# Linear attention and a GELU layer on one core: batch 3 in quarters, batch 2's x later, and four small reads ahead on ScalarE's DMA queue

## The chip, the core and the metric

The kernel runs on one core of a Trainium2 chip. The core has a matrix engine (TensorE, called PE in the profile, with its weight loads in a row of their own, PEld), VectorE (DVE), ScalarE (ACT), GpSimd (POOL) and SyncE (SP). SP issues nearly all DMA transfers; sixteen DMA engines carry them out. The metric is the device time of one execution in microseconds (us). Before the change the median of three runs is 287.24 us (287.09 to 288.22).

## The reference

The inputs q, k and v are [8 batches, 8 heads, 576 rows, 64], the weights are w_in [512, 2048] and w_out [2048, 512], all float32.

```
q_s = softmax(q) over its last axis
k_s = softmax(k) over the 576 rows
kv  = k_s^T v                      # per batch and head, 64 x 64
x   = (q_s kv), heads side by side # 4608 x 512
out = gelu(x w_in) w_out           # exact gelu, 4608 x 512
```

A softmax of numbers drawn at a tenth of a normal needs no maximum subtracted here: the kernel takes exp and divides by the sum.

## The kernel before

**Tiles.** The first 512 rows of a batch are a chunk; the 64 rows that are left of each of the eight batches make a ninth chunk. So there are nine chunks c = 0 to 8 of 512 rows. For each, `h_phase(c)` computes h = x w_in in sixteen groups t of four 128x512 matmuls (L376), each followed by a gelu on ACT (L381) into g. `y_phase(c)` computes g w_out: four output tiles j, each a sum over sixteen t (L386), copied out of PSUM by DVE (L393) and stored by SP. These matmuls are bf16 and keep PE busy; everything else is placed among them.

**What goes in front of a chunk.** `exp_q` and `exp_k` take exponentials on ACT; `table` loads ACT's function table for exp or gelu. `norm_q` divides q by its sums (DVE sums and reciprocals, POOL and DVE products). `xbar_step` transposes q with a DMA issued by SP, into qT (for batches 0 and 1 PE does it). `cast_v_all` turns v into bf16 on DVE. `kv_step` computes k_s^T v on PE for two head pairs and writes it, divided by the sums, into `kvbd[b]`, 128x128 per head pair with the two heads' blocks on the diagonal. Then x = q_s kv is computed transposed, for four head pairs hp:

- `x_step(b, hp)`: one 128x512 matmul against the 128x128 block (L323) and one evacuation from PSUM into xT, by DVE (L356) or, when told "s", by ACT (L358).
- `x_quad(b)`, for batches from QB on: eight matmuls of 64x64 blocks (L346), which work on quarters of PE's array, then four evacuations. It needs neighbouring head pairs in swapped order, so for those batches the exponentials (`exp_heads`) are four instructions instead of one, each for every fourth head. It uses two accumulators of psum_a and both of psum_y.

With QB = 4, batches 2 and 3 use `x_step`, batches 4 to 7 `x_quad`. The ninth chunk (b = B) mixes the remainders of all batches; its q tile holds two batches in each of four slots, and `exp_main` treats the slots of the batches below QB plainly and the others in four instructions.

**Order.** The order of instructions on each engine is written out by hand: `h_phase` and `y_phase` take a table of small pieces of work to issue after a given t, or after a given (j, t). `h_phase` also takes `groups`: {0: 2} lets the first two groups run side by side, so that each part of xT is read twice before the next is needed. Batch 2's attention is issued within y_phase(1), batch 3's norm, cast and transpose (`front3`) in h_phase(2) after t = 0, its kv_steps after t = 8 and 9 and its x_steps after t = 12 to 15. From batch 4 on the kv_steps stand at t = 1 and 2 and the quad at t = 9 of the phase before.

**Start and end.** SP issues the loads in order: q, k and v of batch 0, w_in in ten transfers, w_out, then batches 1 and 2. Meanwhile 30 matmuls on zeros (`warm`) run on PE. The transfers, of whatever queue, take eight completion semaphores in turn, so each waits until the one eight places ahead has landed. The last output tile (`y_last`) is stored in two column ranges, each half by SP and half by ACT; these two are the only transfers on ACT's queue.

Of the kernel before, what the change touches and what calls it, by code (L numbers as in the profile page):

```python
# [8 lines left out]
FP32 = mybir.dt.float32  # L9
BF16 = mybir.dt.bfloat16  # L10
AF = mybir.ActivationFunctionType
# [5 lines left out]
def kernel(  # L17
# [16 lines left out]
    nc = tc.nc  # L34
# [5 lines left out]
    R = S - M  # L40
    HP = H // 2
    NDM = DM // 128
    NDF = DF // 128
    QB = 4
    PW = 2 * D + 1
    PA = 2 * D + 2
    NS = S // 64
# [2 lines left out]
    singles = ctx.enter_context(tc.tile_pool(name="singles", bufs=1))  # L50
# [50 lines left out]
    def load_main(b, name, t, parts=1):  # L101
        f = f32in.tile([128, 2048 if name == "q" else 2560], FP32, tag=name + "f")
        f = f[:, 0:2048].rearrange("p (h f) -> p h f", h=H)
        st[b][name + "f"] = f
        src = t[b, :, 0:M, :].rearrange("h (p j) d -> p h (j d)", j=J)
        n = H // parts
        for i in range(parts):
            nc.sync.dma_start(out=f[:, i * n:(i + 1) * n, :], in_=src[:, i * n:(i + 1) * n, :])  # L108

    def load_pair(b, name, t, parts):  # L110
        f = f32in.tile([128, 2560], FP32, tag=name + "f")
        f = f[:, 0:HP * NS * D].rearrange("p (x f) -> p x f", x=HP)
        st[b][name + "f"] = f
        src = t[b].rearrange("h (p n) d -> (h p) (n d)", n=NS).rearrange("(x q) f -> q x f", q=128)
        n = HP // parts
        for i in range(parts):
            nc.sync.dma_start(out=f[:, i * n:(i + 1) * n, :], in_=src[:, i * n:(i + 1) * n, :])  # L117
# [9 lines left out]
    def load(b):  # L127
        load_main(b, "q", q)
        load_both(b, "k", k)
        load_both(b, "v", v)  # L130
# [11 lines left out]
    def exp_heads(b, dst, src):  # L142

        if b < QB:
            nc.scalar.activation(out=dst, in_=src, func=AF.Exp)  # L145
            return
        for s, u in ((0, 0), (1, 1), (2, 3), (3, 2)):
            nc.scalar.activation(out=dst[:, s::4], in_=src[:, u::4], func=AF.Exp)  # L148

    def exp_main(b, name, parts=1):  # L150
        if name == "q":
            e = attn_sb.tile([128, J, H, D], BF16, tag="eq")
        else:
            e = ek_main[b % 2]
        st[b]["e" + name] = e
        if b == B:
            f = st[b][name + "f"]
            nc.scalar.activation(out=e[:, 0:QB // 2], in_=f[:, 0:QB // 2], func=AF.Exp)
            for s, u in ((0, 0), (1, 1), (2, 3), (3, 2)):
                nc.scalar.activation(  # L160
                    out=e[:, QB // 2:, s::4], in_=f[:, QB // 2:, u::4], func=AF.Exp
                )
            return
        src = st[b][name + "f"].rearrange("p h (j d) -> p h j d", j=J)
        dst = e.rearrange("p j h d -> p h j d")
        n = H // parts
        for i in range(parts):
            exp_heads(b, dst[:, i * n:(i + 1) * n], src[:, i * n:(i + 1) * n])

    def exp_q(b, parts=1):  # L170
        exp_main(b, "q", parts)

    def exp_k(b, parts=1):
        exp_heads(b, ek_r[b % 2][0:R], st[b]["kr"])
        exp_main(b, "k", parts)
# [84 lines left out]
    def kv_step(b, hps):  # L260
# [7 lines left out]
        for hh in range(2):  # L268
            pr = slice(hh * 64, hh * 64 + 64)
            for i in range(n):  # L270

                c = hh ^ (hps[i] % 2 if b >= QB else 0)
                nc.vector.tensor_scalar_mul(  # L273
# [31 lines left out]
    def xbar_step(b):  # L305
        st[b]["qT"] = attn_sb.tile([128, J, HP, 128], BF16, tag="qT", name="qT")
        nc.sync.dma_start_transpose(
            out=st[b]["qT"].rearrange("p j x m -> p (j x) m"),
            in_=st[b]["eq"].rearrange("p j h d -> p (j h d)"),
        )  # L310
    def x_step(b, hp, eng="v"):
        x_mm(b, hp)
        x_evac(b, hp, eng)

    def x_mm(b, hp):

        pool, tag = (psum_y, "y") if b == 0 else (psum_a, "a")
        if hp == 0:
            st[b]["xT"] = attn_sb.tile([128, HP, M], BF16, tag="xT", name="xT")
        ps = pool.tile([128, M], FP32, tag=tag)  # L320
        st[b][f"x{hp}"] = ps
        if b < B:
            nc.tensor.matmul(ps, kvbd[b][:, hp, :], st[b]["qT"][:, :, hp, :], start=True, stop=True)  # L323
        else:
            for bb in range(B):
                cs = slice(bb * R, (bb + 1) * R)
                s2 = slice(bb % 2 * R, (bb % 2 + 1) * R)
                nc.tensor.matmul(
                    ps[:, cs], kvbd[bb][:, hp, :], st[b]["qT"][:, bb // 2, hp, s2],
                    start=True, stop=True,  # L330
                )

    def x_quad(b, engs="vvvv"):


        st[b]["xT"] = attn_sb.tile([128, HP, M], BF16, tag="xT", name="xT")
        for hp in range(HP):
            pool, tag = (psum_a, "a") if hp < 2 else (psum_y, "y")
            st[b][f"x{hp}"] = pool.tile([128, M], FP32, tag=tag, name="ps")
        for half in range(2):  # L340
            for r in range(2):
                for i in range(2):
                    hp = 2 * half + i
                    pr = slice(r * 64, r * 64 + 64)
                    c = slice((r ^ i) * 64, (r ^ i) * 64 + 64)
                    nc.tensor.matmul(  # L346
                        st[b][f"x{hp}"][c, :], kvbd[b][pr, hp, c], st[b]["qT"][pr, :, hp, :],
                        start=True, stop=True,
                    )
        for hp in range(HP):  # L350
            x_evac(b, hp, engs[hp])

    def x_evac(b, hp, eng="v"):
        ps = st[b][f"x{hp}"]
        if eng == "v":
            nc.vector.tensor_copy(out=st[b]["xT"][:, hp, :], in_=ps)  # L356
        else:
            nc.scalar.copy(out=st[b]["xT"][:, hp, :], in_=ps)  # L358

    def h_phase(c, ins, groups={}, pre={}):  # L360


        g = moe_sb.tile([128, NDF, M], BF16, tag="g", bufs=1)
        st[c]["g"] = g
        xT = st[c]["xT"]
        t1 = 0
        while t1 < NDF:
            t0, t1 = t1, t1 + groups.get(t1, 1)
            ts = range(t0, t1)
            pss = [psum_h.tile([128, M], FP32, tag="h", name="ps") for t in ts]  # L370
            for dm in range(NDM):
                if t0 == 0:
                    for f in pre.get(dm, []):
                        f()
                for ps, t in zip(pss, ts):
                    nc.tensor.matmul(  # L376
                        ps, wi_bf[:, dm, t * 128:(t + 1) * 128], xT[:, dm, :],
                        start=(dm == 0), stop=(dm == NDM - 1),
                    )
            for ps, t in zip(pss, ts):  # L380
                nc.scalar.activation(out=g[:, t, :], in_=ps, func=AF.Gelu)  # L381
                for f in ins.get(t, []):
                    f()
# [92 lines left out]
            nc.tensor.matmul(ps, zeros[:, 0:128], zeros, start=True, stop=True)  # L476


    load_main(0, "q", q, 2)
    load_pair(0, "k", k, 2)  # L480
    load_pair(0, "v", v, 4)
# [74 lines left out]
    def y_end(j):  # L556
# [35 lines left out]
        (1, 12): [lambda: kv_step(2, (0, 1))],  # L592
        (2, 2): [lambda: kv_step(2, (2, 3))],
        (1, 15): [lambda: xbar_step(2)],
        (3, 3): [lambda: x_step(2, 0)],
        (3, 6): [lambda: x_step(2, 1)],
        (3, 9): [lambda: x_step(2, 2)],
        (3, 12): [lambda: x_step(2, 3)],
    })


# [1 line left out]
    def back(b, late=False):  # L603
        s = {}
        if b < B:
            s[8 if late else 1] = [lambda: kv_step(b, (0, 1))]
            s[9 if late else 2] = [lambda: kv_step(b, (2, 3))]
        if QB <= b < B:
            s[9] = [lambda: x_quad(b)]
        else:  # L610
            for hp in range(HP):
                s[(12 if late else 8) + hp] = [lambda hp=hp: x_step(b, hp)]
        return s
# [8 lines left out]
    for c in range(2, B + 1):  # L622
        ins = back(c + 1, c == 2) if c < B else {}
        nb = c + 2
        if c == 2:
            ins[0] = [front3]
        elif nb <= B:
            ins.setdefault(0, []).append(
                (lambda nb=nb: load(nb)) if nb < B else (lambda: load_qrest())
            )  # L630
        h_phase(c, ins)
        yi = {}
        if nb <= B:
            exp_q(nb)
            if nb < B:
                exp_k(nb)
            table(AF.Gelu)
            yi[(1, 0)] = [lambda nb=nb: norm_q(nb)]
            if nb == 4:
                yi[(3, 4)] = [lambda: cast_v_all(4)]  # L640
            elif nb < B:
                yi[(0, 8)] = [lambda nb=nb: cast_v_all(nb)]
            yi[(3, 0)] = [lambda nb=nb: xbar_step(nb)]
        y_phase(c, yi)
# [30 lines left out]
```

The softmax here doesn't subtract the row's maximum and nothing guards it: scores larger than these inputs give would overflow.

## Time and profile before

| What | Value |
|---|---|
| median of three runs | 287.24 us (287.09 to 288.22) |
| the profiled execution's own time | 288.38 us |
| its span (first to last instruction) | 286.5 us |
| PE busy | 278.7 us, 97% |
| granted TensorE clock | 1.00 |
| ACT busy | 157.1 us, 55% |
| DVE busy | 120.2 us, 42% |
| HBM read and written | 36.70 MB, 9.44 MB |

The profile is of one execution. Its span leaves 1.9 us of that execution's time outside. A busy time says how long an engine had at least one instruction in hand; PE's matmuls overlap, so its rate is read from the distance of their starts. Where a line names a releaser ("<-"), that is what ended the idle time before the instruction.

### The profile page before, as it was taken

The page shows a single profiled execution, that of the slowest core. Times are in us where ns is not written, and L with a number is a line of the kernel's source. Part 1 is how long each engine was busy: PE and PEld are TensorE (multiplying, and loading weights), DVE is VectorE, ACT ScalarE, POOL GpSimd, SP SyncE. Part 2 cuts the span into 40 slices and gives each one's busy share as a digit, 9 for nine tenths or more (in the row PEclk, how much of TensorE's full clock was granted, in tenths as well). Part 3 has the DMA queues.
Part 4 walks back from the last instruction along what each step waited for, and adds up shares of the span by engine and source line. Part 5 has one row for each costly group of instructions (what it writes and reads, how often), then busy time and mean ns, then how long its engine had stood idle before and what let it go on. Part 6 is the DMA issues. An engine that isn't in the chain of part 4 may idle for free.

```text
span 286.5 us, 3845 instructions
## 1 busy us (share of the span) xinstructions
PE 278.7 (97%) x1507; PEld 131.3 (46%) x1507; DVE 120.2 (42%) x240; ACT 157.1 (55%) x251; POOL 38.5 (13%) x34
## 2 busy tenths in 40 slices
PE   8989999999899999999999999999999999999994
PEld 3534454445345445444544454445444444444443
DVE  7564387128595555345422632363235112110012
ACT  5777684779355843685268625771665165017400
POOL 5730032002020050005000400041002200000000
PEclk9999999999999999999999999999999999999999
DMA  7999999999809929932995189716701600120033
GB/s 233 375 383 385 373 388 296 293 283 244 161 37 251 297 97 233 258 115 76 214 266 146 73 190 264 172 73 160 136 0 72 147 2 0 73 76 0 0 73 76
DMA packets 58465, 50.05 MB, mean 175 GB/s; under 512 B 26576, under 2 KB 48336, under 8 KB 58448
## 3 DMA queue, kind: packets, MB, share of 16 engines
q1 hardware_dynamic: 58288, 49.68, 62.4%
q8 instruction: 12, 0.20, 0.3%
q10 hardware_dynamic: 160, 0.13, 0.1%
q14 instruction: 5, 0.04, 0.0%
HBM read 36.70 MB, written 9.44 MB: 161 GB/s over the span
## 4 chain that ended last, share of the span: by engine, by line
PE 77%; DMA 15%; SPq 2%; DVE 2%; ACT 1%; issue 1%; POOL 0%; ACTq 0%
PE ps L376 39%; PE ps L386 33%; DMA f<-in_v_dram 7%; DMA f<-in_q_dram 4%; DMA w<-in_moe_w_in_dram 3%; DMA qT<-e 2%; PE ps L251 2%; SPq L108 1%; PE ps L408 1%; DVE qsum L241 1%; PE ps L323 1%; PE ps L346 1%; SPq L117 1%; ACT L145 0%; SPq L463 0%
## 5 line engine op out<-in xcount | busy, mean ns | idle before, releaser
L381 ACT ACTIVATE g<-ps 128x512 bf16<-128x512 f32 x144 | 85.7, 597 | 100.0 <-PE ps L376 100.0
L376 PE MATMUL ps<-xT,wi_bf 128*128 128x512 bf16 x576 | 129.9, 379 | 1.0 <-POOL wi_bf L452 0.8
L386 PE MATMUL ps<-wo_bf,g 128*128 128x512 bf16 x560 | 124.0, 379 | 0.0
L376 PEld LDWEIGHTS <-wi_bf 128*128 128x128 bf16 x576 | 55.2, 98 | 66.5 <-issue 2.4
L386 PEld LDWEIGHTS <-g 128*128 128x128 bf16 x560 | 54.6, 98 | 65.8 <-issue 1.0
L393 DVE COPY y_sb<-ps 128x512 f32<-128x512 f32 x35 | 23.8, 686 | 73.2 <-PE ps L386 73.0
L243 POOL TENSOR_TENSOR e<-e,recq 128x1024 bf16<-128x1024 bf16 (+1 forms) x10 | 27.5, 2758 | 176.8 <-DVE recq L242 94.5
L356 DVE CAST xT<-ps 128x512 bf16<-128x512 f32 x33 | 21.6, 687 | 34.7 <-PE ps L346 20.8
L241 DVE TENSOR_REDUCE qsum<-e 128x16 f32<-128x1024 bf16 (+1 forms) x13 | 21.1, 1623 | 6.9 <-ACT e L145 6.7
L224 DVE CAST v_aug<-f 128x512 bf16<-128x512 f32 x24 | 10.3, 429 | 10.2 <-DMA f<-in_v_dram 9.6
L97 ACT ACT_TABLE_LOAD x9 | 11.5, 1283 | 0.9 <-PEq L659 0.7
L273 DVE TENSOR_SCALAR kvbd<-ps,rec 64x64 bf16<-64x64 f32 x48 | 11.6, 281 | 0.7
L476 PE MATMUL ps<-kvbd 128*128 128x512 bf16 x35 | 10.4, 467 | 1.2 <-DVE scr L85 1.2
L145 ACT ACTIVATE e<-f 128x1024 bf16<-128x1024 f32 (+1 forms) x7 | 8.1, 1174 | 4.9 <-DMA f<-in_q_dram 4.9
L182 ACT ACTIVATE ek<-f 64x1152 bf16<-64x1152 f32 x8 | 9.3, 1162 | 2.6 <-DMA f<-in_k_dram 2.5
L148 ACT ACTIVATE e<-f 128x512 bf16<-128x512 f32 x16 | 8.8, 618 | 0.0
L148 ACT ACTIVATE ek<-f 128x512 bf16<-128x512 f32 x16 | 8.7, 614 | 0.0
L251 PEld LDWEIGHTS <-ek 128*128 128x128 bf16 x96 | 6.8, 97 | 3.2 <-ACT ek L145 0.6
L251 PE MATMUL ps<-v_aug,ek 128*128 128x129 bf16 x96 | 8.1, 220 | 0.1
L467 DVE CAST wo_bf<-w 128x2048 bf16<-128x2048 f32 (+1 forms) x5 | 5.1, 1014 | 5.8 <-DMA w<-in_moe_w_out_dram 5.7
L323 PE MATMUL ps<-qT,kvbd 128*128 128x512 bf16 x16 | 6.1, 381 | 1.3 <-DMA qT<-e 0.7
L476 PEld LDWEIGHTS <-kvbd 128*128 128x128 bf16 x35 | 3.9, 116 | 6.7 <-issue 3.3
(53 smaller groups left out, 99.0 us busy)
## 6 DMA issues: line engine op xcount, KB each, us to landing
out_dram<-y_sb SPq DMA_DIRECT2D x32, 256.0 KB, 2.4
f<-in_q_dram SPq DMA_DIRECT2D x6, 1024.0 KB, 8.3
f<-in_k_dram SPq DMA_DIRECT2D x6, 1024.0 KB, 11.7
f<-in_v_dram SPq DMA_DIRECT2D x6, 1024.0 KB, 10.1
w<-in_moe_w_in_dram SPq DMA_DIRECT2D x6, 512.0 KB, 8.3
w<-in_moe_w_out_dram SPq DMA_DIRECT2D x3, 1024.0 KB, 12.1
f<-in_k_dram SPq DMA_DIRECT2D x4, 576.0 KB, 9.1
f<-in_v_dram SPq DMA_DIRECT2D x8, 288.0 KB, 9.4
```

The source lines that it names most:

```text
L97: nc.scalar.activation(out=scr[:, 1:2], in_=scr[:, 0:1], func=func)
L148: nc.scalar.activation(out=dst[:, s::4], in_=src[:, u::4], func=AF.Exp)
L241: nc.vector.reduce_sum(out=qsum, in_=eq[:, :, hs, :], axis=AX.X)
L243: eng.tensor_tensor(out=eq[:, :, hs, :], in0=eq[:, :, hs, :], in1=recq.unsqueeze(3).to_broadcast([128, J, w, D]), op=ALU.mult,)
L251: nc.tensor.matmul(ps, st[b]["ek"][:, j, hs, :].rearrange("p h d -> p (h d)"), v_aug[b % 2][:, j, hp, 0:PW], start=(j == 0), stop=False,)
L273: nc.vector.tensor_scalar_mul(out=kvbd[b][pr, hps[i], c * 64:c * 64 + 64], in0=ps[pr, i, c * (D + 1):c * (D + 1) + D], scalar1=rec[pr, i:i ...
L356: nc.vector.tensor_copy(out=st[b]["xT"][:, hp, :], in_=ps)
L376: nc.tensor.matmul(ps, wi_bf[:, dm, t * 128:(t + 1) * 128], xT[:, dm, :], start=(dm == 0), stop=(dm == NDM - 1),)
L381: nc.scalar.activation(out=g[:, t, :], in_=ps, func=AF.Gelu)
L386: nc.tensor.matmul(ps, st[c]["g"][:, t, j * 128:(j + 1) * 128], wo_bf[:, t, :], start=(t == 0), stop=(t == NDF - 1),)
L393: nc.vector.tensor_copy(out=y_sb, in_=ps)
L476: nc.tensor.matmul(ps, zeros[:, 0:128], zeros, start=True, stop=True)
```

## The change

Four things, and the lines that belong to them:

- QB is 3, so batch 3 uses `x_quad`, at t = 12 of h_phase(2). Its exponentials become four each; the ninth chunk's q is split accordingly (batch 2's half slot plain, batch 3's half slot in four).
- Batch 2's x_steps move within y_phase(1) from (3,3), (3,6), (3,9), (3,12) to (3,6), (3,8), (3,10), (3,12), and the last of them is evacuated by ACT.
- h_phase(2) gets groups={0: 2}.
- Before all other DMA transfers, ACT issues four reads of 16 rows of 8 bytes each, from k, v, w_in and w_out, into a tile that nothing uses.

```diff
-    QB = 4
+    QB = 3
...
         if b == B:
             f = st[b][name + "f"]
-            nc.scalar.activation(out=e[:, 0:QB // 2], in_=f[:, 0:QB // 2], func=AF.Exp)
-            for s, u in ((0, 0), (1, 1), (2, 3), (3, 2)):
-                nc.scalar.activation(
-                    out=e[:, QB // 2:, s::4], in_=f[:, QB // 2:, u::4], func=AF.Exp
-                )
+            nc.scalar.activation(out=e[:, 0], in_=f[:, 0], func=AF.Exp)
+            exp_heads(2, e[0:R, 1], f[0:R, 1])
+            exp_heads(3, e[R:128, 1], f[R:128, 1])
+            exp_heads(4, e[:, 2:4].rearrange("p j h d -> p h j d"),
+                      f[:, 2:4].rearrange("p j h d -> p h j d"))
             return
...
+    touch = singles.tile([16, 4, 2], FP32)
+    for i, a in enumerate((k[0, 0, 0:16, 0:2], v[0, 0, 0:16, 0:2],
+                           moe_w_in[0:16, 0:2], moe_w_out[0:16, 0:2])):
+        nc.scalar.dma_start(out=touch[:, i, :], in_=a)
...
-        (3, 3): [lambda: x_step(2, 0)],
-        (3, 6): [lambda: x_step(2, 1)],
-        (3, 9): [lambda: x_step(2, 2)],
-        (3, 12): [lambda: x_step(2, 3)],
+        (3, 6): [lambda: x_step(2, 0)],
+        (3, 8): [lambda: x_step(2, 1)],
+        (3, 10): [lambda: x_step(2, 2)],
+        (3, 12): [lambda: x_step(2, 3, "s")],
...
-            s[9] = [lambda: x_quad(b)]
+            s[12 if late else 9] = [lambda: x_quad(b)]
...
-        h_phase(c, ins)
+        h_phase(c, ins, groups={0: 2} if c == 2 else {})
```

## The prediction

> **What bounds the kernel now.** I read the page first, then the chain of waits in order of time, then the timeline around each place where that chain leaves TensorE (PE), and last the DMA rate in half-microsecond stretches over the start.
>
> ```profile
> PE 278.7 (97%) x1507; PEld 131.3 (46%) x1507; DVE 120.2 (42%) x240; ACT 157.1 (55%) x251; POOL 38.5 (13%) x34
> ```
>
> PE is busy nearly throughout, so an edit pays only if it takes PE work out or closes a PE gap. Columns of the chain: start, length, what.
>
> ```profile
> 3.35 8.75 DMA f<-in_v_dram
> 12.10 0.02 issue
> 12.12 7.26 DMA w<-in_moe_w_in_dram
> ...
> 70.29 5.36 DMA qT<-e
> 75.65 0.04 issue
> 75.69 0.38 PE ps L323
> ...
> 79.31 7.77 PE ps L376 x36
> ...
> 95.12 13.81 PE ps L386 x64
> 108.93 1.73 PE ps L376 x8
> ...
> 118.70 0.56 PE ps L346 x8
> ...
> 138.35 1.73 PE ps L376 x8
> ```
>
> Up to about 48 us the chain runs through loads, then over PE with one interruption: at 70.29 it waits for batch 2's transposed q. From 79.31 to the end it is PE alone, 13.81/64 = 0.216 us a matmul; what happens off PE there costs nothing while it is in time. The timeline shows the interruption:
>
> ```profile
> 70.29 3.34 SPq L307 DMA_TRANSPOSE qT<-e  x1
> 74.58 0.10 PEld L323 LDWEIGHTS <-kvbd 128*128 128x128 bf16 x1
> 75.69 0.38 PE L323 MATMUL ps<-qT,kvbd 128*128 128x512 bf16 x1 [0.73 <-DMA qT<-e]
> ```
>
> The weights of batch 2's first x matmul are in at 74.58, its turn is 0.216 later at 74.80, and it starts at 75.69: 0.89 us lost, and the only large PE gap after 49 us.
>
> **Batch 2's x, three y matmuls later.** In y_phase(1) the first x moves from (3,3) to (3,6), so 3 x 0.216 = 0.65 us of y work runs inside the wait; 0.24 us of it stays. The steps then have two y matmuls between them, and the last stays at (3,12). Evacuations: an x comes every 3 x 0.216 = 0.65 us and a VectorE (DVE) evacuation takes 0.69, so DVE falls behind by about 0.04 a step; the fourth goes to ScalarE (ACT) at 0.59 (its row for L358). It starts some 0.4 us after its matmul (76.55 to 76.97 for an x of before) and is done 0.2 us after h_phase(2) starts; that phase reads xT's fourth part as its seventh matmul now that its first two groups run together (1.3 us in; alone 0.65). The cost is nothing, and 0.5 us at most if ACT were late. ACT's load grows first, though:
>
> ```profile
> 68.54 1.89 ACT L145 ACTIVATE e<-f 128x2048 bf16<-128x2048 f32 x1
> 70.34 0.61 ACT L145 ACTIVATE ek_r<-f 64x512 bf16<-64x512 f32 x1
> 70.86 1.89 ACT L145 ACTIVATE ek<-f 128x2048 bf16<-128x2048 f32 x1
> ...
> 74.07 0.20 ACT L97 ACTIVATE scr<-scr 128x1 f32<-128x1 f32 x1
> ```
>
> **Batch 3 in quarters.** Its exponentials become four each. The same forms for batch 4 take 2.19, 0.80 (start to start) and 2.17 us, where batch 3's take 1.89, 0.52 and 1.89: +0.86 us. ACT is then free at 75.1 instead of 74.27; its next work, the fourth evacuation, comes at about 77.9. Cover 2.8 us; if it were gone, the first gelu and then PE would slip one for one. The remainder's exponentials (L158, L160) go from 5 to 10, +0.9 us by the same rows, beside 9.03 us in which ACT waits for PE before its next gelu.
>
> On PE four x matmuls of 128x512 become eight of 64x512. Two stages that differ in this alone give the price: from h_phase(2)'s start to h_phase(3)'s is 108.93 - 79.31 = 29.62 us with four x_steps, the next is 138.35 - 108.93 = 29.42 with a quad: **0.20 us saved**. The Trainium skill (TensorEngine Tiling (Array Packing), Theoretical Speedup) gives up to two for each dimension of 64 or less; for eight quarter-array matmuls that is the time of two whole ones, 0.43 us saved and a sum 0.23 us lower. The row decides, since entering and leaving the quarters costs PE about 0.1 us each: 0.20.
>
> The quad stands at t=12, where batch 3's first x stood. Its qT lands at 89.77 and PE reaches that place at 91.66: 1.9 us of cover, which moves with PE because batch 3's norm on DVE starts after the last y_out of y_phase(1). kv_step(3) at 87.08 comes 0.2 us behind the end of DVE's casts (86.86), but needs only the first two of four. The quad takes both y accumulators; its four evacuations run 2.48 us in batch 4's case, so the third is done about 2.3 us after the quad's start, and y_phase(2) wants that buffer 3.2 us after it. No cost; the 0.9 us are the cover.
>
> **The four reads ahead.** They put four issues on ACT before its first table load. SP's issues at the start take 0.45 to 0.51 us, ACT's two at the end average 0.73; I take 0.55, the shorter of ACT's two. So the table load moves from 0.73 to about 2.9, and the dummy exponential ends at 4.4, just ahead of q's first half (exponential at 4.63). With 0.8 each it would be at 5.4, 0.8 us late; behind it stand DVE's sum and POOL's product (done at 9.26), and PE's transposes wait for the warm-up matmuls until 9.99, so 0.7 us of that is covered. The transfers share eight completion semaphores in turn: v's four loads on SP now wait for the four reads to land, with all weight loads behind them. The first weight load waited for q's first half (4.61) before, too, and the rings hold q and k up to about 8 us, so there are some 3 us of cover.
>
> What can they gain? The first k packets meet something slow (columns: stretch, busy of PE, PEld, DVE, ACT, POOL, clock, DMA share, GB/s):
>
> ```profile
> 4.50:5.00 0.50, 0.50 (x3) 0.15 (x2) 0.45 (x2) 0.37 (x1) 0.02 (x1) 1.00 1.13 365
> 5.00:5.50 0.50, 0.50 (x3) 0.22 (x2) 0.41 (x3) 0.50 (x1) 0.00 (x0) 1.00 1.08 250
> 5.50:6.00 0.50, 0.50 (x3) 0.22 (x2) 0.43 (x2) 0.19 (x1) 0.00 (x0) 1.00 0.88 265
> ```
>
> The engines are busy and move a third less. Against 380 GB/s the stretches from 5.0 to 6.5 lack about 0.35 us of transfer and the one from 7.5 to 8.0 0.09. Single k packets in the trace take 0.4 to 1.1 us instead of 0.09, and of the sixteen completion marks of k's first load fifteen come by 8.02 and the last at 9.10: one DMA engine stays 1.1 us behind, and every load to 44 us lands by it. v and the weights show no such packets at their first use, so two or three of the four reads have little to gain. If the k read absorbs the stall, loads land 0.45 (mean) to 1.1 us (last engine) sooner. Through the start this is worth less: the q chain (warm-up to 9.99, then DVE's evacuation, v cast, norms, x evacuation) is bound by no load. Replacing k, v and w_in landings by ones 1.1 us earlier and walking the timeline, the point from which h_phase(0) runs without gaps moves from 18.16 to about 17.7: 0.45 us; a gap of 0.29 us at 47.17, where batch 1's last v part comes late, goes as well. PE then reaches batch 2's x 0.74 us sooner and finds the same transpose: its packets start at 71.5, halt from 72.8 to 73.5 while the last engines finish batch 3's load (last v mark 73.20), and land at 75.65. That landing moves only with the DMA engines. So of the start's gain I count what the rings gain, the mean **0.45**, not 0.74. Bounds: -0.3 (the reads stand in q's way) and +0.98 (0.74 plus the 0.24 still waited at x).
>
> Against this speaks the Trainium skill (DMA: Bandwidth & Descriptors, Issuing engines are not separate DMA queues): ACT's and SP's transfers run on the same sixteen engines and interleave. Whoever reads k first, the engine waits; by that rule the stall moves from 5 us to 2.5 us, into q's landing, and the reads give 0: 286.2. By the rows it could be hidden there, since q's own ramp moves only 184 GB/s from 2.0 to 2.5 us. I side with the rows, narrowly.
>
> **The end.** Both last output pairs are issued at 282.58:
>
> ```profile
> 282.58 1.17 SPq L417 DMA_DIRECT2D out_dram<-y_sb  x2
> 282.58 1.45 ACTq L417 DMA_DIRECT2D out_dram<-y_sb  x2
> ```
>
> These are ACT's first transfers; their data starts at 284.2, SP's at 283.7, and the last landings are 285.43 and 285.26. If that is the queue's first use, the reads pay it earlier: **0.17 us**, 0 otherwise.
>
> **Sum.** 0.65 + 0.20 + 0.45 + 0.17 = 1.47 us. The profiled execution took 288.38 us (span 286.5, 1.9 around it), so it would be 286.9. It lies 1.1 above the median of the runs shown; nothing in the sum lies outside the span, so the same microseconds come off that: 287.24 - 1.47 = **285.8**, or 0.51%.
>
> **Rivals.** (a) The reads change nothing at the start: 0.65 + 0.20 + 0.17 = 1.02, 286.2 (286.4 without the end). For it: the shared engines, and v and weights that need no warming. Against it: 1.1 us packets at k's first use alone. (b) The transpose lands so early that x never waits, because its 70.29 issue rides with PE and the slow engine is gone: 0.74 + 0.89 + 0.20 + 0.17 = 2.0, 285.2. For it: later transposes land 4.7 to 4.8 us after issue, this one 5.36. Against it: a second engine is 0.9 us behind after an instruction fetch at 18.24 and stays so. (c) Slower: the four reads each hold every DMA engine like k's worst packets, one after another, with q behind them. Up to four times 1 us on q; 0.7 is covered, and the three other gains are 1.02, so it loses from q landing 1.7 us late; at 4 us the time is 287.24 + 3.3 - 1.02 = 289.5. Against it: v and the weights start without long packets. (d) The quad or the exponentials don't fit and PE waits: it takes more than 0.9 or 2.8 us of delay, and the forms are measured; with it the time is near 287.
>
> **How the numbers follow.** Main case 0.45, (a) 0.26, (b) 0.20, (c) 0.05, (d) 0.04. A measurement of this kernel tells about 0.5% (1.44 us, 285.80) from no change. The main case lies on that bound and gives a little over half of its chance, 0.25, to faster (its own range is 285.4 to 286.2); (b) gives 0.20, (a) 0.04: faster 0.49. Slower: most of (c) and a little of (d), 0.06. The rest, 0.45, is within. The range runs from (b) less 0.2 us to (a) with 0.4 us of loss at q: 285.0 to 286.8; it leaves (c), (d) and the tails out.
>
> **What would show it.** Right: x's wait at L323 in y_phase(1) short or gone, with 0.65 us more y work ahead of it; k's first exponential at about 8 us instead of 9.13; the stage of h_phase(2) at 29.4; ACT's last data as early as SP's. Wrong: k's exponential still at 9.1, or q's later than 4.63 by over 0.7; the transpose landing later than 75.65; a wait at L346 or before y_phase(2).

## The result, and the profile after

| | Before | After |
|---|---|---|
| median of six runs each, side by side | 287.94 us (287.09 to 288.39) | 286.31 us (285.99 to 287.01) |
| ratio after/before, 95% interval | | 0.9951 (0.993 to 0.9972) |
| repeated in a larger set of runs | 287.38 us | 286.65 us, 0.9977 (0.9967 to 0.9986) |
| profiled execution: its time, its span | 288.38 us, 286.5 us | 286.36 us, 284.4 us |

The change makes the kernel faster. The first measurement gives 0.49%, where 0.51% was forecast; the repetition, with a narrower interval, gives 0.23%, less than half. The median of 286.31 us is 0.5 above the forecast 285.8, inside its range. The two profiled executions differ by 2.0 us, more than either ratio, so part of that difference belongs to these two executions and not to the kernels. Much of what follows is about that.

On the page of after, PE's row of busy time, share of the span and instructions:

```profile
PE 276.6 (97%) x1484; PEld 131.1 (46%) x1511; DVE 119.4 (42%) x239; ACT 159.7 (56%) x266; POOL 38.6 (14%) x34
```

(Some matmul records are missing from this trace, so PE's count is below PEld's. The weight loads are complete: 1511, where before had 1507.)

The chain of waits of after in order of time (start, length, what):

```profile
1.19 9.04 PE ps L476 x30
10.23 0.46 PE ps L288 x8
...
17.68 9.44 PE ps L376 x43
...
71.87 2.97 PE ps L386 x13
74.84 0.21 PE ps L323
75.05 0.43 PE ps L386 x2
...
77.64 4.96 PE ps L376 x23
...
90.00 0.56 PE ps L346 x8
...
107.07 1.73 PE ps L376 x8
...
136.49 1.73 PE ps L376 x8
```

Three things are to be seen. Up to 10.23 the chain now stands on the warm-up matmuls and the first transposes instead of on v's load; h_phase(0) runs without gaps from 17.68. The DMA wait of 5.36 us ahead of batch 2's first x is gone: the y matmuls run straight into L323. And batch 3's part of the phase is a quad (L346 at 90.00): from h_phase(2)'s start at 77.48 in the timeline to h_phase(3)'s at 106.90 is 29.42 us, where before had 29.62. The stage after it (107.07 to 136.49 in the chain) has 29.42 too.

The timeline of after around batch 2's x:

```profile
67.77 2.17 ACT L148 ACTIVATE e<-f 128x512 bf16<-128x512 f32 x4
...
69.52 2.93 SPq L307 DMA_TRANSPOSE qT<-e  x1
...
69.85 0.89 ACT L148 ACTIVATE ek_r<-f 64x128 bf16<-64x128 f32 x4
...
70.65 2.17 ACT L148 ACTIVATE ek<-f 128x512 bf16<-128x512 f32 x4
...
74.13 0.20 ACT L97 ACTIVATE scr<-scr 128x1 f32<-128x1 f32 x1
74.46 0.10 PEld L323 LDWEIGHTS <-kvbd 128*128 128x128 bf16 x1
74.67 0.38 PE L323 MATMUL ps<-qT,kvbd 128*128 128x512 bf16 x1
...
77.03 0.59 ACT L358 CAST xT<-ps 128x512 bf16<-128x512 f32 x1 [2.70 <-PE ps L323]
```

The weights are in at 74.46 and the matmul starts 0.21 later: no wait. The transpose is issued 0.77 sooner than before (69.52, was 70.29) and lands 4.4 us later, at 73.9 (before: 5.36, at 75.65). The exponentials end at 72.8 and ACT is free at 74.33, 2.7 us before it evacuates the fourth x.

The last stores of after:

```profile
280.72 1.11 SPq L417 DMA_DIRECT2D out_dram<-y_sb  x2
280.72 1.38 ACTq L417 DMA_DIRECT2D out_dram<-y_sb  x2
```

From this issue to the end of the span it is 3.72 us; before it was 3.88.

In this pair of executions the 2.1 us of span split up as follows: h_phase(1) starts 0.69 earlier (46.98, was 47.67), the stage with x is 0.96 shorter (30.51, was 31.47), the quad gives 0.20, the end 0.16, which is 2.01; rounding makes the rest.

### The profile page after: what moved, and what is told of

It is laid out like the page before. It is cut to its first block, busy times and chain, and to the rows that moved or that the text cites. A ratio compares the mean times of both kernels' runs of the same rounds, so it can differ in the third digit from the quotient of the medians.

```text
span 284.4 us, 3842 instructions
## 1 busy us (share of the span) xinstructions
PE 276.6 (97%) x1484; PEld 131.1 (46%) x1511; DVE 119.4 (42%) x239; ACT 159.7 (56%) x266; POOL 38.6 (14%) x34
## 4 chain that ended last, share of the span: by engine, by line
PE 91%; DMA 3%; DVE 2%; ACT 2%; issue 1%; DVEq 0%; ACTq 0%
PE ps L376 40%; PE ps L386 40%; PE ps L476 3%; DMA f<-in_k_dram 3%; PE ps L251 2%; PE ps L408 1%; PE ps L346 1%; PE ps L323 1%; DVE xT L356 1%; ACT ek L145 1%; DVE kvbd L212 1%; PE ps L197 1%; PE ps L255 0%; PE ps L288 0%; ACT L145 0%
## 5 line engine op out<-in xcount | busy, mean ns | idle before, releaser
L376 PE MATMUL ps<-xT,wi_bf 128*128 128x512 bf16 x560 | 128.6, 379 | 1.3 <-DVE xT L356 0.3
L356 DVE CAST xT<-ps 128x512 bf16<-128x512 f32 x32 | 20.6, 686 | 32.6 <-PE ps L346 22.5
L148 ACT ACTIVATE e<-f 128x512 bf16<-128x512 f32 (+2 forms) x28 | 13.2, 540 | 0.1
L148 ACT ACTIVATE ek<-f 128x512 bf16<-128x512 f32 x20 | 10.9, 613 | 0.0
L145 ACT ACTIVATE e<-f 128x1024 bf16<-128x1024 f32 (+1 forms) x7 | 6.8, 990 | 3.2 <-DMA f<-in_q_dram 3.2
L216 DVE CAST vr_aug<-f 64x512 bf16<-64x512 f32 x6 | 2.5, 416 | 8.7 <-DMA f<-in_v_dram 8.7
```

Of the source, the lines that this page charges most:

```text
L376: nc.tensor.matmul(ps, wi_bf[:, dm, t * 128:(t + 1) * 128], xT[:, dm, :], start=(dm == 0), stop=(dm == NDM - 1),)
```

## The experiments

Two theories stood against each other. **S (stall)**: the reads take over what k's first packets meet, so k and everything behind it lands sooner and the start is shorter. **I (issue)**: what the reads touch is of no account; that four more transfers go first changes when later ones run, and the gain, if any, comes with that. Beside these, each part of the change was made alone.

### Each part alone

The reads alone, with everything else as before:

```diff
+    touch = singles.tile([16, 4, 2], FP32)
+    for i, a in enumerate((k[0, 0, 0:16, 0:2], v[0, 0, 0:16, 0:2],
+                           moe_w_in[0:16, 0:2], moe_w_out[0:16, 0:2])):
+        nc.scalar.dma_start(out=touch[:, i, :], in_=a)
```

> The kernel before with the four reads alone. Theory S (k's first use stalls the DMA engines; with the reads ahead no engine stays behind, so the transpose of batch 2's q is no longer late): the start is 0.77 us shorter by the end of h_phase(1), the transpose lands by 74 us, batch 2's x at (3,3) starts with hardly any wait, h_phase(2) starts about 1.6 us earlier than the 79.14 of before; 1.7 to 1.9 us off the time, with 0.1 at the end. Rival R (the transpose was early for another reason, the later x or the quarters): only the 0.77 us of the start, x then waits 0.9 to 1.7 us, 0.1 to 0.8 us off the time.

Measured: 287.21 us beside 287.29, ratio 0.9988 (0.9974 to 1.0002). The interval ends at 0.75 us off the time, so S's 1.7 to 1.9 us did not come.

The whole change without the reads (the lines above taken out of after):

> The changed kernel without the four reads. S: k's first exponential at about 9.1 us, one DMA engine late from there on, the transpose lands at about 75.6, x at (3,6) waits 0.24 us; 0.65 + 0.20 = 0.85 us off the time, no gain at the end. R: the transpose lands about 74, no wait; 1.1 us off.

Measured: 287.09 us, 0.9975 (0.9963 to 0.9987).

Batch 2's x later, alone:

```diff
-        (3, 3): [lambda: x_step(2, 0)],
-        (3, 6): [lambda: x_step(2, 1)],
-        (3, 9): [lambda: x_step(2, 2)],
-        (3, 12): [lambda: x_step(2, 3)],
+        (3, 6): [lambda: x_step(2, 0)],
+        (3, 8): [lambda: x_step(2, 1)],
+        (3, 10): [lambda: x_step(2, 2)],
+        (3, 12): [lambda: x_step(2, 3, "s")],
...
-        h_phase(c, ins)
+        h_phase(c, ins, groups={0: 2} if c == 2 else {})
```

> The kernel before with batch 2's x steps later, the fourth evacuation on ACT and the grouped start of h_phase(2). S and R: 0.65 us off, 0.24 us of the wait left, h_phase(2) starts at 78.5 instead of 79.14. If the wait had grown by what the x steps were moved (the transpose held up by the same work), nothing is gained.

Measured: 287.23 us, 1.0000 (0.9987 to 1.0014).

Batch 3 in quarters, alone:

```diff
-    QB = 4
+    QB = 3
...
+            nc.scalar.activation(out=e[:, 0], in_=f[:, 0], func=AF.Exp)
+            exp_heads(2, e[0:R, 1], f[0:R, 1])
+            exp_heads(3, e[R:128, 1], f[R:128, 1])
...
-            s[9] = [lambda: x_quad(b)]
+            s[12 if late else 9] = [lambda: x_quad(b)]
```

> The kernel before with batch 3 in quarters alone (x steps of batch 2 where they were, no reads). Both theories: 0.20 us off, all of it between h_phase(2)'s and h_phase(3)'s start (29.62 to 29.42 us); ACT free at 75.1 instead of 74.27 with no wait behind it.

Measured: 287.00 us, 0.9991 (0.9979 to 1.0004).

Of these four only the combination without the reads is apart from no change by its interval; the parts alone are too small for the measurement. By time alone the reads add nothing that can be seen: 0.9975 without them here, 0.9977 with them in the repetition of the whole change, another set of runs. The traces say more. One row per kernel, all from single profiled executions: the landings of k's and v's first part, PE's first transposes (L288, their start in the timeline; the chain above counts them from the end of the piece before), h_phase(1)'s start, the stage from there to h_phase(2) (30.50 is its length without any wait at x), the next stage, the landing of batch 3's last v load, the transpose of batch 2's q from issue to landing, and from the last stores' issue to the end.

| Kernel | k | v | L288 | h_phase(1) | stage with x | next stage | batch 3's v | transpose | end |
|---|---|---|---|---|---|---|---|---|---|
| before | 9.10 | 11.35 | 10.21 | 47.67 | 31.47 | 29.62 | 73.20 | 5.36 | 3.88 |
| quad_only | 9.53 | 11.78 | 9.43 | 47.83 | 30.50 | 29.42 | 71.98 | 4.33 | 3.80 |
| before_pad8 | 8.63 | 10.88 | 9.29 | 47.57 | 30.60 | 29.62 | 72.25 | 4.56 | 3.81 |
| x_later_only | 8.31 | 10.57 | 9.43 | 46.77 | 30.51 | 29.62 | 71.04 | 4.34 | 5.47 |
| x_later_pad8 | 8.30 | 10.56 | 9.33 | 46.71 | 31.14 | 29.62 | 72.55 | 5.75 | 3.80 |
| no_touch | 8.23 | 10.48 | 9.30 | 46.53 | 31.22 | 29.42 | 72.43 | 5.83 | 3.82 |
| no_touch_w26 | 8.33 | 10.58 | 9.29 | 47.37 | 30.51 | 29.42 | 72.42 | 4.95 | 3.81 |
| after | 8.15 | 10.41 | 10.07 | 46.98 | 30.51 | 29.42 | 71.35 | 4.37 | 3.72 |
| after_again | 8.02 | 10.25 | 10.35 | 47.27 | 30.50 | 29.42 | 70.27 | 4.39 | 3.70 |
| touch_only | 8.21 | 10.46 | 10.52 | 47.43 | 30.51 | 29.62 | 70.17 | 4.38 | 3.71 |
| after_w28 | 8.03 | 10.30 | 9.34 | 47.20 | 30.51 | 29.42 | 70.34 | 4.38 | 3.72 |
| after_w26 | 8.44 | 10.71 | 9.31 | 47.54 | 30.51 | 29.42 | 70.73 | 4.39 | 3.73 |
| after_reads_of_q | 8.05 | 10.27 | 9.62 | 47.21 | 30.51 | 29.42 | 70.55 | 4.38 | 3.71 |
| after_reads_of_k | 8.61 | 10.87 | 10.03 | 46.94 | 30.52 | 29.42 | 70.75 | 4.38 | 3.75 |

(The kernels further down in the table are those of the next parts. The first seven make no reads, the last seven do.)

The quad shows in every row: 29.42 with it, 29.62 without. The stage with x does not behave as a property of the kernel: in the seven without reads it is 30.50 to 31.47, and moving x doesn't decide it. The timeline of no_touch, with x at its later place, still waits:

```profile
69.08 3.82 SPq L307 DMA_TRANSPOSE qT<-e  x1
...
74.95 0.38 PE L323 MATMUL ps<-qT,kvbd 128*128 128x512 bf16 x1 [0.55 <-DMA qT<-e]
```

and that of touch_only, with x at its old place, does not (no idle time in the brackets; the transpose has landed at 74.36, x starts at 74.49):

```profile
69.98 1.86 SPq L307 DMA_TRANSPOSE qT<-e  x1
...
74.49 0.38 PE L323 MATMUL ps<-qT,kvbd 128*128 128x512 bf16 x1
```

PE comes to x about 4.5 us after the transpose is issued at the old place (quad_only 74.88 - 70.37, touch_only 74.49 - 69.98) and about 5.15 us at the later one (after 74.67 - 69.52), the difference being the 0.65 us of y work. So x waits for what the transpose takes beyond 4.5, or beyond 5.15. With reads it took 4.4 in all seven profiles, and neither place has to wait. Without them it took 4.33 to 5.83.

Two columns of the table say what makes it long. In all fourteen profiles the transpose lands, to 0.04 us, at the later of two times: 4.36 us after its own issue, and 2.45 us after batch 3's last v load has landed. Before: 73.20 + 2.45 = 75.65, as measured. no_touch: 72.43 + 2.45 = 74.88 (landed at 74.91). After: 69.52 + 4.36 = 73.88 (73.89), where v gives only 73.80. touch_only: 69.98 + 4.36 = 74.34 (74.36). So a late transpose is one that stands behind batch 3's load. With reads that load is done early enough in all seven for the issue to count; without them it is so only in quad_only and x_later_only.

### Do the reads work through k's first use?

In after the DMA rate over k's first packets is this (stretch, busy of PE, PEld, DVE, ACT, POOL, clock, DMA share, GB/s):

```profile
4.50:5.00 0.50, 0.50 (x2) 0.15 (x1) 0.45 (x2) 0.35 (x1) 0.03 (x1) 1.00 1.10 381
5.00:5.50 0.50, 0.50 (x3) 0.22 (x2) 0.41 (x3) 0.50 (x1) 0.00 (x0) 1.00 1.25 341
5.50:6.00 0.50, 0.50 (x3) 0.23 (x2) 0.41 (x2) 0.20 (x1) 0.00 (x0) 1.00 0.96 318
```

341 and 318 where before had 250 and 265: taken alone, a confirmation of S. The same kernel in another execution (after_again) takes it back:

```profile
5.00:5.50 0.50, 0.50 (x3) 0.22 (x2) 0.40 (x3) 0.50 (x1) 0.00 (x0) 1.00 0.89 200
5.50:6.00 0.50, 0.50 (x3) 0.23 (x2) 0.42 (x2) 0.19 (x1) 0.00 (x0) 1.00 0.86 269
```

Two runs test S further: the four reads all of q, which is loaded first anyway, and the read of k alone.

```diff
-    for i, a in enumerate((k[0, 0, 0:16, 0:2], v[0, 0, 0:16, 0:2],
-                           moe_w_in[0:16, 0:2], moe_w_out[0:16, 0:2])):
+    for i, a in enumerate((q[0, 0, 0:16, 0:2], q[0, 1, 0:16, 0:2],
+                           q[0, 2, 0:16, 0:2], q[0, 3, 0:16, 0:2])):
```

> The changed kernel with all four small reads from q instead of k, v and the weights: the same number of transfers on ACT's queue, and the same waits of SP's v loads for them, but nothing of k, v or the weights is touched. S (first use of k): as without the reads; last mark of k's first load between 8.2 and 9.6, v's first part from 10.5 on, batch 3's loads complete at 71 to 73.2. Theory I (what counts is that SP's loads are issued in smaller steps, since v's loads wait for the reads): as with the reads; k by 8.2, v by 10.5, batch 3's loads by 70.2 to 71.4, no wait at x.

Measured: 286.59 us beside 287.25, 0.9964 (0.9949 to 0.9979); the change itself had 0.9951 and 0.9977, in other sets of runs. Its stretches:

```profile
5.00:5.50 0.50, 0.50 (x3) 0.25 (x2) 0.41 (x3) 0.50 (x1) 0.00 (x0) 1.00 1.16 245
5.50:6.00 0.50, 0.50 (x4) 0.24 (x3) 0.47 (x2) 0.11 (x1) 0.00 (x0) 1.00 0.91 254
```

```diff
-    for i, a in enumerate((k[0, 0, 0:16, 0:2], v[0, 0, 0:16, 0:2],
-                           moe_w_in[0:16, 0:2], moe_w_out[0:16, 0:2])):
+    for i, a in enumerate((k[0, 0, 0:16, 0:2],)):
```

> The changed kernel with the one read of k alone. S: as with all four reads, k's first load complete by 8.2 and v's first part by 10.5. I: only one of v's loads waits for a read, so it is nearer to the kernel without the reads: v's first part from 10.5 to 11.8.

Measured: 286.76 us, 0.9973 (0.9960 to 0.9987).

S falls. With reads of q the rate over k's first packets is as low as in before (245 and 254), yet k and v land at 8.05 and 10.27, among the earliest in the table, the transpose takes 4.38 and the gain in time is no smaller than in the repetition. With k's read alone k and v land at 8.61 and 10.87, later than with any other set of reads. And the rate itself does not follow the reads: no_touch, with no read at all, moved 312 and 336 GB/s there, while after_again, after_w28 and after_w26, which all read k first, moved 200, 213 and 153 in the first of the two stretches. The slow stretch is a matter of the execution. Packets of k that take 0.4 us or more are in the traces with the reads too (0.4 to 1.4 us, at 4.9 to 5.9).

I is left, but not in the form that it was given. What goes with the reads in all seven profiles is a transpose of 4.4 us and batch 3's last v at 70.2 to 71.4 (71.0 to 73.2 without), and packets of 1,024 bytes between 47 and 70 us that take 58 to 63 ns in the mean instead of 64 to 68. One read has it as well as four. That speaks against the number of transfers too, and leaves something that all these kernels share. One such thing is the reads' own tile: its 32 bytes per partition push every later tile by 32 bytes, and in the built programs the tiles that the loads fill then start at multiples of 64 bytes where they stood 32 past one. Against it speak the later loads into the same tiles: between 86 and 110 us packets of 1,024 bytes take 57 to 64 ns without reads and 57 to 62 with them. A kernel with such a tile and no reads, or with reads and a tile of 64 bytes, would tell; neither was run, so what makes batch 3's load land sooner stays open.

### The change repeated, and eight small matmuls

x_later_only had an end of 5.47 us, against 3.7 to 3.9 for all others. In its trace a transfer of 16,384 bytes on the queue that fetches instructions starts at 282.38, takes 1.2 us of one DMA engine, and lies among the last stores. Such fetches come every 18 to 32 us, and the idea (theory F below) is that the number of instructions decides where the last one falls. The quad has eight PE instructions more than the x_steps (four matmuls and four weight loads). To move the fetch alone, four matmuls of 64 columns on zeros were put behind the warm-up at the first transposes (with their weight loads, also eight), in before and in x_later_only; the change itself ran again beside them.

```diff
-    def warm(n):
+    def warm(n, small=0):
...
+        for i in range(small):
+            nc.tensor.matmul(ps[:, 0:64], zeros[:, 0:128], zeros[:, 0:64], start=True, stop=True)
...
-    warm(5)
+    warm(5, 4)
```

> The kernel before with four matmuls of 64 columns behind the second warm-up, in a stretch in which PE waits: eight more PE instructions (weight loads counted), as many as the quarters add. Theory F (the last 16 KB instruction fetch of PE falls among the last output transfers in the kernels with the old number of PE instructions, and holds one DMA engine for over 1 us): the last fetch comes 2 to 4 us ahead of the end of PE instead of beside it, and the time falls by 0.1 to 0.3%. Rival: the number of instructions does not matter, same time to 0.1%.

> The later x steps alone, with the same eight PE instructions. F: its gain of 0.65 us, which showed in the places of its timeline but not in its time (1.0000), comes out: 0.997 to 0.998. Rival (the later x gains nothing because the transpose is late or not by chance): 0.9995 to 1.0005 again.

> The changed kernel once more, beside many runs of the kernel before. Theory S (the reads keep an engine from falling behind): k's first load again complete by 8.3 us, no wait at x, ratio about 0.995, and better than without the reads (0.9975) by 0.2% or so. Theory L (luck: the late engine is an event of single executions, which the reads do not touch): some executions late as in before; ratio no better than 0.9975 - within 0.1%.

Measured, beside 287.38: before_pad8 287.12 us, 0.9979 (0.9964 to 0.9995); x_later_pad8 286.88, 0.9975 (0.9964 to 0.9986); after_again 286.65, 0.9977 (0.9967 to 0.9986). Time from issue to landing of the last four stores, x_later_only:

```profile
DMA to landing us min/median/max: 2.1/3.7/4.0
```

and x_later_pad8:

```profile
DMA to landing us min/median/max: 2.0/2.1/2.4
```

In x_later_pad8 the last fetch is at 278.1, 3.2 us before the stores are issued at 281.3. Added work of no use makes these kernels about 0.2% faster, as much as the whole change in the repetition. An instruction fetch moved out of the end fits that, and one was caught in x_later_only's trace. It is not shown for the kernel before, though: its fetch at 281.1 was over when the stores' data moved, its end of 3.88 us isn't long, and quad_only, with eight more instructions too, measured 0.9991. Nor does the number alone decide it: touch_only and no_touch_w26 have as many PE instructions as before and show no such fetch after 251.4 us at all. Why the added work helps is open. The repetition of the change fits theory S in its landings (k at 8.02, no wait at x) and theory L in its ratio, 0.9977 where S had about 0.995. The later x adds nothing here: 0.9975 against 0.9979.

### The warm-up matmuls

In after the chain begins with the 30 warm-up matmuls, and the first transposes wait for them. Two or four fewer should then start everything sooner.

```diff
-    warm(30)
+    warm(28)
```

> The changed kernel with 28 instead of 30 warm-up matmuls ahead of the first transposes; in its profile these 30 are what the start waits for (1.19 to 10.2 us) while q is normalised by 9.3. If so, the first gapless h_phase comes 0.4 us earlier and the time falls by up to 0.15% against the changed kernel. If PE's clock falls back for want of two matmuls, or the weights' landing (14.2 us) is the next bound, nothing is gained or it is slower.

> The changed kernel with 26 warm-up matmuls. In ten profiles so far the end of the stop-and-go start is the later of two things: the first transposes (behind the 30 warm-ups) + 7.6 us, and the landing of v's first part + 6.75 us. With the four reads v's part landed at 10.25 to 10.46, and the warm-ups ended late enough to be what counted in the three profiles with 30 of them. With 26 the transposes follow q's norm (9.3 us) in every execution, so h_phase(0) runs without gaps from 17.0 to 17.2 instead of 17.7 to 18.1, and the time falls by 0.1 to 0.3% against the changed kernel, to 0.995 to 0.997. If the clock falls back, or the gain is lost at x, no change (0.998).

> The same without the four reads. Theory S: now nothing hides the loads; v's first part lands between 10.5 and 11.8, the start is 0.2 to 1.4 us longer than in the kernel with the reads, the transpose is late in some executions; 0.1 to 0.3% slower than after_w26. Theory L: the reads do nothing, the same time to 0.1%.

(after_w26 has warm(26), no_touch_w26 the same without the reads.) Measured: after_w28 286.53 us beside 287.38, 0.9969 (0.9956 to 0.9982); after_w26 286.92 beside 287.25, 0.9982 (0.9965 to 0.9998); no_touch_w26 287.07, 0.9991 (0.9975 to 1.0007). The timeline of after_w28:

```profile
1.19 7.79 PE L476 MATMUL ps<-kvbd 128*128 128x512 bf16 x28 [1.19 <-DVE scr L85]
9.34 0.62 PE L288 MATMUL ps<-identity,e 128*128 128x128 bf16 x8 [0.37 <-POOL e L243]
...
20.27 0.61 PE L376 MATMUL ps<-xT,wi_bf 128*128 128x512 bf16 x2 [0.30 <-DVE wi_bf L456]
...
43.40 0.38 PE L197 MATMUL ps<-v_aug,ek 128*128 128x65 bf16 x7 [0.21 <-POOL v_aug L188]
```

The transposes now wait for POOL's product of q instead (0.37 at 9.34), 0.73 earlier than in after, and h_phase(0) runs from 17.01 instead of 17.68. But PE then runs into the weights (0.30 at 20.27) and into batch 1's v (0.21 at 43.40), and h_phase(1) starts at 47.20, no sooner than after's 46.98. after_w26 missed its forecast: v landed at 10.71, later than assumed, h_phase(0) ran without gaps from 17.47 instead of 17.0 to 17.2, and the ratio is not below the change's. The intervals of all these lie over each other; no version here is shown to beat the change, and with 26 warm-ups the reads' gain (0.9982 against 0.9991) isn't apart from nothing.

## Why the prediction was right, and where it was not

**Batch 3 in quarters, 0.20: right.** 29.62 against 29.42 in every profile. Its side claims held too: exponentials of 2.17, 0.89 and 2.17 us, no wait at L346 and none before y_phase(2). ACT was free at 74.33, even sooner than the 75.1 counted, since they began sooner.

**Batch 2's x later, 0.65: the mechanism is right, the size is that of one execution.** The 0.89 us of before is what the transpose took beyond 4.5 us in that execution; quad_only and before_pad8, with the same place of x, lost 0 and 0.10, so the three lost 0.36 in the mean (their stages less 30.50: 0.97, 0, 0.10). Taking the seven landings without reads, and supposing that they don't depend on the place, x waits 0.56 us in the mean at the old place and 0.21 at the new one: worth 0.35 by that estimate. The four profiles with x at the new place and no reads do not bear it out: they lost 0.35 in the mean, as much as the three at the old place. In time no gain was seen (1.0000; 0.9975 against 0.9979), and with the reads nothing is left to gain, since touch_only has no wait at the old place. The fourth evacuation by ACT cost nothing, as counted.

**The reads, 0.45: the number is near, its cause is wrong.** The step that failed is "If the k read absorbs the stall, loads land 0.45 (mean) to 1.1 us (last engine) sooner". Loads do land sooner with reads, by 0.41 us for k (mean of seven 8.22, without 8.63) and 0.42 for v (10.47, without 10.89); but reads of q do it as well, and k's read alone least. And the 0.45 doesn't come out at the start: h_phase(1) starts at 47.22 in the mean with reads and at 47.21 without. The walk to a gapless h_phase(0) from 17.7 was exact for after (17.68), and v's landing had ruled in before (11.35); but in the other profiles without reads and with x later v came at 10.5 and the same point was 17.2 to 17.4. What goes with the reads is at x. The transpose takes 4.4 us in all seven profiles, which saves the wait: 0.35 us in the mean of the seven without reads. "That landing moves only with the DMA engines" was right for before, where batch 3's load held the transpose up; once that load is out of the way the landing moves with the issue, which comes sooner when PE does (69.52, was 70.29). That the engines are freer at 70 us because of something at 5 us was not borne out. After's own execution is rival (b): x without a wait, and its sum of 2.0 us is what this pair of profiles shows.

**The end, 0.17: half of it, and not by the way forecast.** From the last stores' issue to the end it is 3.70 to 3.75 us with reads and 3.80 to 3.88 without (x_later_only left out): 0.10. But an earlier use of ACT's queue did not bring ACT's data forward. ACT's last landing comes 0.17 us after SP's in before, in no_touch and in after alike, and its data starts 1.56 us after its issue in no_touch and in after (before: 1.63). What is shorter is the time from the last landing to the end of the span: 1.02 to 1.03 us in all seven without reads, 0.93 to 0.97 in the seven with them. In the traces four of SP's closing waits, about 0.06 us apart, end after the last landing in every profile without reads, and three in every profile with them: the reads take away one wait at the very end, one read as well as four.

**ACT and SP at the start: no cost, as counted.** ACT's four issues take 0.43 to 0.45 each, not 0.55 (and ACT's two at the end of before average 0.68, not 0.73); its table load starts at 2.63 and q's first exponential at 4.65, where it was 4.63. SP's last v loads wait for the reads to land, so v's four issues end at 6.6 us instead of 4.7 and the first weight load goes out at 7.41 instead of 4.78; h_phase(0) in after waits for neither. So (c) did not happen, and (d) did not either.

**The sum.** With the terms that the profiles show (the quad, x's mean wait without reads, the end), 0.20 + 0.35 + 0.10 = 0.65 us, or 0.23%: near what the repetition measured (0.73 us between the medians, 0.9977), and less than the first measurement (1.63 us, 0.9951). Against the measured 0.49% the forecast of 0.51% looks better than its steps were: 0.65 for x was taken from an execution in which the wait was at its largest. What is left over of the first measurement, some 0.3%, is not explained by any wait in the traces; part of it is the small sample, since the six runs of before had a median of 287.94 us and its three larger sets, of 67 to 75 runs, 287.25 to 287.38. That the first ratio met the forecast so closely is in good part luck. And since eight matmuls and weight loads of no use gave 0.9979, the time of the repetition alone couldn't tell the change's own gain from theirs; the 0.65 rests on the traces, one execution of each kernel.

## What to carry to other kernels

A wait for a DMA in one profile is one drawing: before it is priced, ask for its margin (here the landing after 4.3 to 5.8 us against the moment of use after 4.5 or 5.15) and for its size in other executions. A transfer that is issued behind a load has two clocks, its own issue and that load's landing; find out which of them counts. When a cause is suspected in what a transfer touches, let it touch something else, and look at a second execution: the reads of q and a repeat of the same kernel refuted what one matching trace seemed to confirm. And when an effect is as small as 0.2%, run the kernel with a few instructions of no use beside it: here eight of them were worth as much, for a reason that isn't shown.

## What the hardware showed beyond that

**The warm-up's pace.** The warm-up matmuls follow each other at 0.43 us and from some moment on at 0.216. The first one at the new pace starts at 6.5 us in before, 6.2 in after, 7.1 in touch_only, 4.5 in after_w28, 4.1 in no_touch and before_pad8: over all fourteen profiles 2.9 to 5.9 us after the first warm-up at 1.19. The Trainium skill (TensorE: Matmul & The Clock Gate, Part 1: The HAM clock gate) gives two clocks with a ratio of two, and a window of 3.4 us that doesn't start with the kernel, with a transition about 4 us into the work, give or take 0.5; the ratio agrees, the spread here is wider, and the profile's granted clock reads 1.00 throughout. It matters because 30 matmuls last until 10.2 us with a late change: the start is then bound by PE. In all fourteen profiles the time from which h_phase(0) runs without gaps agrees to 0.1 us with the later of two, the first transposes plus 7.61 us and v's first landing plus 6.75: after 10.07 + 7.61 = 17.68, touch_only 10.52 + 7.61 = 18.13, quad_only 11.78 + 6.75 = 18.53, x_later_only 10.57 + 6.75 = 17.32. In the five profiles with reads and 30 warm-ups the first counts (in after_reads_of_k by 0.02), so the sooner v was of no use there. Nothing in the reads touches PE, and with 28 and 26 warm-ups and reads the change of pace came at 4.5 and 4.1; that it was late (5.3 to 7.1) in those five is taken for chance, which these runs don't show.

**Instruction fetches.** Each 16,384-byte transfer occupies one DMA engine for 0.9 to 1.9 us in these traces. Where one fell among stores that use all sixteen engines, in x_later_only, the slowest of them landed 4.0 us after its issue instead of 2.4, and the kernel's end was 1.6 us later.
